# Two linear-attention and MLP layers on one core: the key chain regrouped, POOL's products held, norm turns moved into projections

## Chip, core and metric

The kernel runs on one core of a Trainium2 chip. The metric is the device time of one execution in microseconds (us); lower is better. Before the change the median of three executions is 2591.75 us (2591.71 to 2595.26).

Engines are called PE (TensorE, matmul; its weight loads are a row of their own, PEld), DVE (VectorE), ACT (ScalarE), POOL (GpSimd) and SP (SyncE, which issues the DMAs). PSUM holds matmul results, SBUF everything else. "L521" is line 521 of the kernel before; in the changed kernel the same statement stands 1 to 18 lines further down.

## Reference

The input x is 2048 x 576. Two layers with the same weights; 32 heads of width 18; the MLP is 4608 wide.

```python
def attention(x):                                  # x: [1, 2048, 576]
    q, k, v = heads(x @ wqkv)                      # each [1, 32, 2048, 18]
    pq, pk = q @ w_phi, k @ w_phi                  # per head, 18 x 18
    phi_q = concat([softmax(pq), softmax(-pq)])    # 36 features
    phi_k = concat([softmax(pk), softmax(-pk)])
    kv = phi_k^T v ; z = sum over rows of phi_k    # not causal: over all rows
    o = (phi_q kv) / (phi_q z + 1e-6)
    return merge(o) @ wo

def mlp(x):
    r = max(x @ w1 + b1, 0)
    return (r * r) @ w2 + b2

for _ in range(2):
    x = x + attention(layernorm(x))
    x = x + mlp(layernorm(x))
```

Since kv and z are sums over all rows, no query can be finished before the last key of its layer.

## The kernel before

**Arithmetic.** Every fp32 operand of a matmul is cut into a high and a low piece ("h" and "l": hi is the value cast, lo the rest), and a product is three matmuls: hi hi, hi lo, lo hi. The cuts are the small casts and subtractions on ACT, DVE and POOL throughout.

**Tiles.** The rows come in 4 blocks of 512 (TB), a block in 4 tiles of 128 rows; layer 0 has 16 key tiles K0 to K15. A projection of a tile is made in two halves of 288 columns (`half`).

**Order.** The program order on each engine is the order in which the code issues. Most stages fill a `Plan`: `plan.on(slot, depth, call)`; the slots are run in turn, and within a slot the calls of greater depth first. A slot is roughly one half projection of PE (14 matmuls). The barrier is written out by hand.

**Opening.** First `Fold` multiplies the feature weights w_phi into wqkv (`turn` = PE transposes L215 into "fp" and copies "ft", `times` = products "fo" L228, five chunks c), and `values` cuts the value weights of a chunk: hi on ACT (L254), lo on POOL (L255). Between these the first four row tiles get layer norm: `stats` (DVE bn_stats, then three small POOL operations L355, L356, L335 that make the scale and the shift), `scale` (ACT L344 and L345, which write the normed rows n_0n and n_0e) and `turn` (PE transposes L380 and L389, then cut into n_0h and n_0l by L381 and L382).

Then come the key tiles. For each T: two halves of k (PE, copied by ACT L445 into raw keys `ks`), `Keys.soften`, two halves of v, and `add`, the product kv += phi_k^T v (PE "kvp", L521), which needs the scaled exponentials of T. `soften` is five calls: peaks (DVE max and min, L457 and L458, and for T < 12 the second half of the difference on POOL, L471), difference (DVE L471), exponential (ACT L481), normalisers (DVE sum L484 and reciprocal L485), scale (DVE L494). Its table `at` gives slot and depth of each. The norm of the row tile four tiles ahead runs in the same slots, and in some of them `PrepareO` cuts the output weights ("or", "oh": ACT L296, DVE L297).

**Barrier** (`barrier`, once per layer). After the last key: the sums over heads are spread by matmuls (`key_totals`: "z", copied by ACT into zb) and kv is put into block form (`key_blocks`: transposes "kt", DVE products "ko", cut into kbh and kbl by `key_pieces`). Meanwhile PE projects queries of another block (`halves[1]` to `[7]`). The queries of four tiles Q0 to Q3 are then divided by their totals, two at a time, by `Weights`: `product` (E times zb, L594), `total` (sum, L599), `both` (L604 to L607, four small operations), `apply` (L494, scales E). The first pair is all on DVE, the second pair has its products on POOL. `heads` transposes the scaled queries (PE L630, "t0opt") and multiplies them by the key blocks (L651); `project` multiplies by wo (L674), and DVE adds to x (L677). Then the layer norm of the four tiles, whose transposed pieces (t0onh, t0onl in layer 0; t1onh, t1onl in layer 1) feed the MLP.

**MLP** (`g_mlp`, a generator; each `next(gen)` runs it up to its next `yield`). Feature block f of 128: `first` and `first2` bring weights (in the very first block of layer 0 raw, cut by ACT L765/L777 and POOL or DVE L766/L778), `hidden` is x @ w1 (L799), `square`, `second` (L817, L825). In the block behind a barrier ("apart") `hidden` is run on the first half of the rows (two tiles) before the other half is normed.

Of the kernel before, what the change touches and what calls it, by code (L numbers as in the profile page):

```python
# [7 lines left out]
F32 = mybir.dt.float32  # L8
# [5 lines left out]
P = 128  # L14
TB = 512
NT = TB // P
# [5 lines left out]
def layers_kernel(  # L22
# [78 lines left out]
    class Plan:  # L101
# [44 lines left out]
    nc.vector.tensor_copy(zero.rearrange("p (a b) -> p a b", a=2),  # L146
                          ident[0:1, P // 2 :].unsqueeze(1).to_broadcast([1, 2, P // 2]))
    zeros = zero[:, : 2 * DH].unsqueeze(1).to_broadcast([1, NS, 2 * DH])
    mhalf = cst.tile([P, 1], F32, name="mhalf")
    nc.vector.memset(mhalf, -0.5)  # L150
    b1t = cst.tile([P, NF], F32, name="b1t")
# [16 lines left out]
    class Fold:  # L168
# [81 lines left out]
        def values(self, c):  # L250
            for half in range(2):
                hi, lo = (piece[:, c] for piece in self.vpair[half])
                raw = self.vraws[c][:, half * HP : (half + 1) * HP]
                nc.scalar.activation(hi, raw, AF.Copy)  # L254
                nc.gpsimd.tensor_sub(lo, raw, hi.bitcast(F32))  # L255


# [290 lines left out]
    def key_blocks(layer):  # L548
        kv = sums[layer]["kv"]
        last, w = NG - 1, gw[-1]  # L550
        kbh = cst.tile([GW, 2, D], F32R, name=f"kbh{layer}", tag="kbh")
        kbl = cst.tile([GW, 2, D], F32R, name=f"kbl{layer}", tag="kbl")
        sums[layer]["kb"] = kbh, kbl
        own = sb.tile([P, KC * P], F32, tag="xn", name=f"kq{layer}")
        own = own[:, : 2 * w].rearrange("p (s q f) -> p s q f", s=2, q=NQ)
        nc.vector.tensor_mul(own, kv[:, :, HG].unsqueeze(2).to_broadcast([P, 2, NQ, DH]),
                             quarter.unsqueeze(1).unsqueeze(3).to_broadcast([P, 2, NQ, DH]))
        blocks, todo = own, []
        for s in range(2):
            pt = wtile(f"kt{layer}{s}")  # L560
            nc.tensor.transpose(pt[:GW, :P], kv[:, s, :HG].rearrange("p j f -> p (j f)"), ident)
            own = sb.tile([P, TB], F32, tag="hr", name=f"ko{layer}{s}", bufs=2)
            own = own[:GW, : NQ * GW].rearrange("p (q j d) -> p q j d", q=NQ, j=HG)
            src = pt[:GW, :P].rearrange("p (q d) -> p q d", q=NQ)[:, :, 1 : 1 + DH]
            nc.vector.tensor_mul(own, src.unsqueeze(2).to_broadcast([GW, NQ, HG, DH]),
                                 mask.unsqueeze(1).unsqueeze(3).to_broadcast([GW, NQ, HG, DH]))
            todo.append((own.rearrange("p q j d -> p (q j d)"), [k[:, s, : last * GW] for k in (kbh, kbl)]))
        pt = wtile(f"kt{layer}2")
        p3 = pt[:w, : 2 * w].rearrange("p (s n) -> p s n", s=2)
        for s in range(2):  # L570
            nc.tensor.matmul(p3[:, s], blocks[:, s].rearrange("p q f -> p (q f)"),
                             place.rearrange("p q d -> p (q d)"), start=True, stop=True)
        todo.append((p3, [k[:w, :, last * GW :] for k in (kbh, kbl)]))
        return todo

    def key_pieces(todo):
        for own, (hi, lo) in todo:
            nc.scalar.activation(hi, own, AF.Copy)
        for own, (hi, lo) in todo:
            nc.vector.tensor_sub(lo, own, hi.bitcast(F32))  # L580

# [165 lines left out]
    def g_mlp(layer, b, x, after, name, fresh, apart):  # L747
# [89 lines left out]
        if apart:  # L837
            for f in range(2):
                first(f, nc.gpsimd)
                first2(f, nc.gpsimd)  # L840
            yield
            for f in range(2):
                hidden(f, halves[0])
            yield
            for f in range(2):
                hidden(f, halves[1])
                square(f)
            yield
# [94 lines left out]
    class Keys:  # L943
# [41 lines left out]
        def add(self, T):  # L985
            kv_tile(self.layer, self.vts.pop(T), self.e.pop(T), f"{self.name}kv{T}")

        def soften(self, plan, T, raw, shared, at=((1, 1), (2, 2), (3, 3), (4, 4), (5, 5))):
            plan.on(raw + at[0][0], at[0][1], self.peaks, T, shared)
            for call, (k, depth) in zip((self.differences, self.exponential, self.normalisers, self.scale), at[1:]):  # L990
                plan.on(raw + k, depth, call, T)

    def barrier(layer, b, keys, queries, other, dst, out, gen):

        halves = [lambda t=t, h=h: other.half(t, h) for t in range(NT) for h in range(2)]
        keys()
        halves[1]()
        key_totals(layer)
        halves[2]()
        todo = key_blocks(layer)  # L1000
        weights = [Weights(layer, ([queries.e[t] for t in ts], queries.r[:, ts.start : ts.stop]),
                           f"{out.name}w{ts.start}") for ts in (range(0, 2), range(2, NT))]
        w = weights[0]
        w.product(0)
        w.total(0)
        halves[3]()
        w.product(1)
        key_pieces(todo)
        w.total(1)
        halves[4]()  # L1010
        w.both()
        halves[5]()
        w.apply(0)
        halves[6]()
        w.apply(1)
        halves[7]()
        out.ph = [queries.e[t] for t in range(NT)]
        for t in range(NT):
            out.load(t)
        w = weights[1]  # L1020
# [12 lines left out]
        next(gen)  # L1033
        w.total(0)
        w.total(1)
        out.project(0)
        w.both()
        w.apply(0)
        w.apply(1)
        out.project(1)  # L1040
        heads(1, 2)
        for t in range(2):
            norm.stats(t, out.x[t])
            norm.shift(t)
            norm.scale_by_act(t)
        for t in range(2, NT):
            out.project(t)
            norm.stats(t, out.x[t])
            norm.shift(t)
        spare["tags"] = [f"acc{i}" for i in range(NC)]  # L1050
        for t in range(2):
            norm.turn(t)
        norm.rest(0)
        for t in range(2, NT):
            norm.scale_by_act(t)
        next(gen)
        for t in range(2, NT):
            norm.turn(t)
        norm.rest(1)
        spare["tags"] = []  # L1060

# [7 lines left out]
    def opening():  # L1069
# [53 lines left out]
        for N in range(NT):  # L1123
            plan.on(3 * N + 1, 2, stats, N)
            plan.on(3 * N + 3, -1, scale, N)
            plan.on(3 * N + 4, -2, turn, N)
        for c, slot in enumerate((3, 5, 7, 9, 11)):
            plan.on(slot, -2, fold.values, c)
        first = NK - 2
# [215 lines left out]
```

## Time and profile before

| | us |
|---|---|
| median of 3 executions | 2591.75 |
| profiled execution | 2592.06 |
| its span, first to last instruction | 2590.1 |
| PE busy | 2529.3 |
| DVE busy | 1175.1 |
| ACT busy | 741.8 |
| POOL busy | 108.9 |

The mean granted clock of PE is 0.996 of full speed. Layer 0's opening fold fills about the first 30 us, the key tiles the stretch from 30 to 215, its barrier 213 to 271; layer 1's barrier is at about 1490 to 1550. The rest is MLP and the attention of other blocks woven into it, where PE is busy nearly throughout.

In a list of waits a row reads: engine, its waiting instruction's output and line, "<-" the engine, output and line that came last, then us in total, times, longest. In a timeline a row is start, duration, engine, line, operation, out<-in with shapes; in brackets the idle time of that engine just before, and what ended it.

### The profile page before, as it was taken

The numbers are of one execution on the slowest core, as the hardware profiler recorded it, in microseconds if no ns is written. First come the engines' busy times: TensorE is split into PE (matmuls) and PEld (weight loads), VectorE is DVE, ScalarE is ACT, GpSimd is POOL, SyncE is SP. The second block draws the span as 40 slices with busy tenths as digits, with TensorE's granted clock in tenths as the row PEclk, the third lists the DMA queues.
The fourth block names the chain that finished last, engine by engine and source line by source line (L and its number), as shares of the span: only waits on it lengthen the run. The fifth ranks groups of instructions, "written<-read, shape, count | busy, mean of one in ns | idle before, by whom it ended". The sixth has DMA issues, their size and how long they took to land.

```text
span 2590.1 us, 37314 instructions
## 1 busy us (share of the span) xinstructions
PE 2529.3 (98%) x15300; PEld 2222.6 (86%) x15300; DVE 1175.1 (45%) x1985; ACT 741.8 (29%) x1278; POOL 108.9 (4%) x261
## 2 busy tenths in 40 slices
PE   8888999999999999999999989999999999999999
PEld 8888788888888888888888978888888888888887
DVE  5678775444543445434312676332263326332112
ACT  5433443422221222312222332212222222222221
POOL 3211000000000000000000010000000000000000
PEclk9999999999999999999999999999999999999999
DMA  9404586886656766565566217556654674556655
GB/s 316 155 20 142 188 278 222 276 306 230 199 199 209 240 239 200 165 224 186 184 196 210 100 51 231 162 180 223 226 164 145 193 267 153 164 175 227 197 194 172
DMA packets 161143, 505.47 MB, mean 195 GB/s; under 512 B 21334, under 2 KB 49526, under 8 KB 160974
## 3 DMA queue, kind: packets, MB, share of 16 engines
q1 hardware_dynamic: 160974, 503.10, 58.4%
q8 instruction: 121, 1.98, 0.3%
q14 instruction: 48, 0.39, 0.0%
HBM read 418.39 MB, written 84.64 MB: 194 GB/s over the span
## 4 chain that ended last, share of the span: by engine, by line
PE 85%; DVE 6%; ACT 2%; DMA 2%; issue 1%; POOL 1%; SPq 0%; DVEq 0%; ACTq 0%
PE m_1ph L799 9%; PE m_0ph L799 9%; PE m_2ph L799 9%; PE m_3ph L799 7%; PE m_1acc L825 7%; PE m_0acc L825 7%; PE m_2acc L825 7%; PE m_3acc L825 6%; PE m_1acc L817 2%; PE m_0acc L817 2%; PE m_2acc L817 2%; PE m_3acc L817 2%; DMA m_3rr<-in_B_w 2%; PE a_2po L674 1%; PE a_0po L674 1%
## 5 line engine op out<-in xcount | busy, mean ns | idle before, releaser
L799 PE MATMUL m_0ph<-a_0nh,m_0h 128*128 128x512 f32 x720 | 226.2, 396 | 0.0
L799 PE MATMUL m_2ph<-a_2nh,m_2h 128*128 128x512 f32 x720 | 225.5, 395 | 0.3 <-DMA m_2h<-dw 0.3
L825 PE MATMUL m_3acc<-m_3s,m_3hb 128*128 128x448 f32 x864 | 189.6, 367 | 0.4 <-DVE m_3hb L809 0.4
L825 PE MATMUL m_1acc<-m_1s,m_1hb 128*128 128x448 f32 x864 | 189.5, 367 | 0.4 <-PE m_1ph L799 0.4
L825 PE MATMUL m_0acc<-m_0s,m_0hb 128*128 128x448 f32 x864 | 189.9, 368 | 0.0
L825 PE MATMUL m_2acc<-m_2s,m_2hb 128*128 128x448 f32 x864 | 189.6, 367 | 0.0
L825 PEld LDWEIGHTS m_1acc<-m_1s,m_1hb 128*128 128x128 f32 x864 | 161.6, 188 | 18.3 <-PE m_1ph L799 0.5
L825 PEld LDWEIGHTS m_3acc<-m_3s,m_3hb 128*128 128x128 f32 x864 | 161.3, 188 | 17.8 <-PE m_3ph L799 0.6
L825 PEld LDWEIGHTS m_2acc<-m_2s,m_2hb 128*128 128x128 f32 x864 | 160.6, 188 | 16.0
L809 DVE CAST m_2hb<-m_2hr 128x512 fp32r<-128x512 f32 x72 | 30.8, 427 | 315.9 <-ACT m_2hr L806 315.5
L825 PEld LDWEIGHTS m_0acc<-m_0s,m_0hb 128*128 128x128 f32 x864 | 160.3, 188 | 15.5
L799 PEld LDWEIGHTS m_2ph<-a_2nh,m_2h 128*128 128x128 f32 x720 | 135.3, 188 | 31.1 <-issue 0.7
L799 PEld LDWEIGHTS m_0ph<-a_0nh,m_0h 128*128 128x128 f32 x720 | 135.3, 188 | 29.9
L809 DVE CAST m_1hb<-m_1hr 128x512 fp32r<-128x512 f32 x72 | 30.7, 427 | 270.1 <-ACT m_1hr L806 270.1
L805 ACT ACTIVATE m_2hr<-m_2ph,b1t 128x512 f32<-128x512 f32 x72 | 49.6, 689 | 351.9 <-PE m_2ph L799 351.9
L809 DVE CAST m_0hb<-m_0hr 128x512 fp32r<-128x512 f32 x72 | 30.8, 427 | 260.8 <-ACT m_0hr L806 260.4
L805 ACT ACTIVATE m_0hr<-m_0ph,b1t 128x512 f32<-128x512 f32 x72 | 49.6, 689 | 333.4 <-PE m_0ph L799 333.4
L805 ACT ACTIVATE m_1hr<-m_1ph,b1t 128x512 f32<-128x512 f32 x72 | 49.6, 689 | 324.2 <-PE m_1ph L799 324.2
L799 PE MATMUL m_3ph<-t0onh,m_3h 128*128 128x512 f32 (+1 forms) x380 | 116.3, 390 | 6.7 <-ACT m_3hr L805 3.9
L799 PE MATMUL m_1ph<-t1onh,m_1h 128*128 128x512 f32 (+1 forms) x380 | 114.2, 384 | 1.0 <-ACT t1onh L381 1.0
L799 PE MATMUL m_3ph<-a_3nh,m_3h 128*128 128x512 f32 x360 | 113.1, 396 | 0.0
L799 PE MATMUL m_0ph<-a_0nl,m_0h 128*128 128x512 f32 x288 | 113.0, 392 | 0.0
(1930 smaller groups left out, 5506.9 us busy)
## 6 DMA issues: line engine op xcount, KB each, us to landing
m_2h<-dw SPq DMA_DIRECT2D x72, 640.0 KB
m_0h<-dw SPq DMA_DIRECT2D x72, 640.0 KB
m_1h<-dw SPq DMA_DIRECT2D x72, 640.0 KB
m_2s<-dw SPq DMA_DIRECT2D x72, 576.0 KB
m_0s<-dw SPq DMA_DIRECT2D x72, 576.0 KB
m_1s<-dw SPq DMA_DIRECT2D x72, 576.0 KB
dw<-m_3h SPq DMA_DIRECT2D x36, 640.0 KB
m_3h<-dw SPq DMA_DIRECT2D x36, 640.0 KB
```

Of the source, the lines that this page charges most:

```text
L674: nc.tensor.matmul(pt[:, :HP], a, m[:w, g], start=(g == 0 and k == 0), stop=(g == NG - 1 and k == 2))
L799: nc.tensor.matmul(ph[:, cols], a, m, start=(k == 0), stop=(k == 3 * KC + 1))
L805: nc.scalar.activation(hr, ph, AF.Relu, bias=b1t[:, f : f + 1])
L809: nc.vector.tensor_copy(hh, hr)
L817: nc.tensor.matmul(acc[KC], a, m, start=(f == 0 and k == 0), stop=(f == NF - 1 and k == 2))
L825: nc.tensor.matmul(acc[t][:, :R], a[:, rows], m, start=(f == 0 and k == 0), stop=(f == NF - 1 and k == 2))
```

## The change

1. `Keys.soften` has another table: the difference directly behind the peaks in the same slot, and the exponential, normalisers and scale ahead of the other work of their slots, the scale one slot earlier. `between` (layer 1) uses the same table.
2. In the opening fold `values` casts hi on POOL too (before: ACT), and each norm turn comes one slot later.
3. In the barrier `key_blocks` is issued before `key_totals`, apart from its last part (`own_blocks`), which follows them; `key_pieces` is split: `key_highs` (ACT) after the first total, `key_lows` (DVE, kbl) between the two `apply` calls. `apply(0)` is issued before `halves[5]`.
4. `hold(e)` copies one column of e to a tile `gate` on POOL. Since e is written by `apply`, POOL's later instructions start only after that `apply`. It stands before the second pair's products and before the first MLP step, and that step (`next(gen)`) moves from before `total(0)` of the second pair to after its `apply(1)`.
5. At the barrier's end, turn(0) and turn(1) of the norm stand between the two halves of `project(3)`, turn(2) between the two `hidden` calls of the MLP's first half of rows, turn(3) after them.

```diff
+    gate = cst.tile([P, 1], F32, name="gate")
...
-                nc.scalar.activation(hi, raw, AF.Copy)
+                nc.gpsimd.tensor_copy(hi, raw)
                 nc.gpsimd.tensor_sub(lo, raw, hi.bitcast(F32))
...
         blocks, todo = own, []
+
+        def own_blocks():
...
+            todo.append((p3, [k[:w, :, last * GW :] for k in (kbh, kbl)]))
+            return todo
+
         for s in range(2):
             pt = wtile(f"kt{layer}{s}")
...
-        return todo
-
-    def key_pieces(todo):
+        return own_blocks
+
+    def key_highs(todo):
         for own, (hi, lo) in todo:
             nc.scalar.activation(hi, own, AF.Copy)
+
+    def key_lows(todo):
         for own, (hi, lo) in todo:
             nc.vector.tensor_sub(lo, own, hi.bitcast(F32))
...
             for f in range(2):
                 hidden(f, halves[0])
-            yield
+                yield
...
-        def soften(self, plan, T, raw, shared, at=((1, 1), (2, 2), (3, 3), (4, 4), (5, 5))):
+        def soften(self, plan, T, raw, shared, at=((1, 2), (1, 1.5), (2, 3), (3, 4), (4, 5))):
...
+    def hold(e):
+        nc.gpsimd.tensor_copy(gate, e[:, 0, 0:1])
...
         halves[1]()
+        own_blocks = key_blocks(layer)
         key_totals(layer)
+        todo = own_blocks()
         halves[2]()
-        todo = key_blocks(layer)
...
         w.product(0)
         w.total(0)
+        key_highs(todo)
         halves[3]()
         w.product(1)
-        key_pieces(todo)
         w.total(1)
         halves[4]()
         w.both()
+        w.apply(0)
         halves[5]()
-        w.apply(0)
+        key_lows(todo)
+        w.apply(1)
         halves[6]()
-        w.apply(1)
         halves[7]()
...
+        hold(queries.e[1])
         w = weights[1]
         w.product(0, nc.gpsimd)
         w.product(1, nc.gpsimd, True)
...
         norm = Norm(dst, f"{out.name}n")
-        next(gen)
         w.total(0)
         w.total(1)
         out.project(0)
         w.both()
         w.apply(0)
         w.apply(1)
+        hold(queries.e[3])
+        next(gen)
         out.project(1)
         heads(1, 2)
...
-        for t in range(2, NT):
-            out.project(t)
-            norm.stats(t, out.x[t])
-            norm.shift(t)
+        out.project(2)
+        norm.stats(2, out.x[2])
+        norm.shift(2)
         spare["tags"] = [f"acc{i}" for i in range(NC)]
+        out.project(3, (0,))
         for t in range(2):
             norm.turn(t)
+        out.project(3, (1,))
         norm.rest(0)
-        for t in range(2, NT):
-            norm.scale_by_act(t)
+        norm.scale_by_act(2)
+        norm.stats(3, out.x[3])
+        norm.shift(3)
+        norm.scale_by_act(3)
         next(gen)
-        for t in range(2, NT):
-            norm.turn(t)
+        norm.turn(2)
+        next(gen)
+        norm.turn(3)
         norm.rest(1)
...
-            plan.on(3 * N + 4, -2, turn, N)
+            plan.on(3 * N + 5, -2, turn, N)
```

What this makes of the order on DVE around key tile K4 (s0K4m holds its peaks, s0K4e the differences and exponentials, n_1 and n_2 are the norms of row blocks 1 and 2), before:

```order
L457 TENSOR_REDUCE s0K4m<-s0ks_1170 128x32
L458 TENSOR_REDUCE s0K4m<-s0ks_1170 128x32
L382 TENSOR_TENSOR n_1l<-n_1p_1237,n_1h 128x4x128
L391 TENSOR_TENSOR n_1h<-n_1p_1244,n_1h 64x256
L353 BN_STATS n_2s_1253<-x_8_995 128x6 x2
L354 BN_AGGR n_2m_1254<-n_2s_1253 128x2
L471 TENSOR_TENSOR s0K4e<-s0ks_1170,s0K4m 128x576
L297 TENSOR_TENSOR or_928<-or_928,oh_1206 72x288
L484 TENSOR_REDUCE s0K4r<-s0K4e 128x64
L485 RECIPROCAL s0K4r<-s0K4r 128x64
L494 TENSOR_TENSOR s0K4e<-s0K4e,s0K4r 128x1152
```

and now:

```order
L458 TENSOR_REDUCE s0K4m<-s0ks_1174 128x32
L459 TENSOR_REDUCE s0K4m<-s0ks_1174 128x32
L472 TENSOR_TENSOR s0K4e<-s0ks_1174,s0K4m 128x576
L383 TENSOR_TENSOR n_1l<-n_1p_1239,n_1h 128x4x128
L392 TENSOR_TENSOR n_1h<-n_1p_1246,n_1h 64x256
L354 BN_STATS n_2s_1256<-x_8_997 128x6 x2
L355 BN_AGGR n_2m_1257<-n_2s_1256 128x2
L298 TENSOR_TENSOR or_930<-or_930,oh_1208 72x288
L485 TENSOR_REDUCE s0K4r<-s0K4e 128x64
L486 RECIPROCAL s0K4r<-s0K4r 128x64
L495 TENSOR_TENSOR s0K4e<-s0K4e,s0K4r 128x1152
```

The difference of K4 stands directly behind its peaks, ahead of the norm's n_1l and statistics n_2s; the tail of "or" stands ahead of the sum in both.

DVE in barrier 0, from the key blocks to the scaling of Q1, before:

```order
L565 TENSOR_TENSOR ko_3003<-kt_3001,mask 126x504
L565 TENSOR_TENSOR ko_3007<-kt_3005,mask 126x504
L594 TENSOR_TENSOR t0ow0m_3012<-t0q3Q0e,zb_2961 128x1152
L599 TENSOR_REDUCE t0ow0u<-t0ow0m_3012 128x64
L594 TENSOR_TENSOR t0ow0m_3032<-t0q3Q1e,zb_2961 128x1152
L580 TENSOR_TENSOR kbl_2998<-ko_3003,kbh_2997 126x504
L580 TENSOR_TENSOR kbl_2998<-ko_3007,kbh_2997 126x504
L580 TENSOR_TENSOR kbl_2998<-kt_3009,kbh_2997 72x2x72
L599 TENSOR_REDUCE t0ow0u<-t0ow0m_3032 128x64
L604 TENSOR_TENSOR t0ow0u<-t0ow0u,t0q3r 128x128
L605 SCALAR_TENSOR_TENSOR t0ow0u<-t0ow0u 128x2x32
L606 RECIPROCAL t0ow0u<-t0ow0u 128x2x32
```

and now:

```order
L601 TENSOR_TENSOR t0ow0m_3013<-t0q3Q0e,zb_2974 128x1152
L606 TENSOR_REDUCE t0ow0u<-t0ow0m_3013 128x64
L601 TENSOR_TENSOR t0ow0m_3036<-t0q3Q1e,zb_2974 128x1152
L606 TENSOR_REDUCE t0ow0u<-t0ow0m_3036 128x64
L611 TENSOR_TENSOR t0ow0u<-t0ow0u,t0q3r 128x128
L612 SCALAR_TENSOR_TENSOR t0ow0u<-t0ow0u 128x2x32
L613 RECIPROCAL t0ow0u<-t0ow0u 128x2x32
L614 TENSOR_TENSOR t0q3r<-t0q3r,t0ow0u 128x128
L495 TENSOR_TENSOR t0q3Q0e<-t0q3Q0e,t0q3r 128x1152
L587 TENSOR_TENSOR kbl_2963<-ko_2968,kbh_2962 126x504
L587 TENSOR_TENSOR kbl_2963<-ko_2972,kbh_2962 126x504
L587 TENSOR_TENSOR kbl_2963<-kt_2993,kbh_2962 72x2x72
```

The three subtractions into kbl left the place between the products of Q0 and Q1 and their sums; they stand behind the scaling of Q0.

POOL in barrier 0, from the products of the second pair to the cuts of the MLP's first weights (m_3h, m_3s), before:

```order
L594 TENSOR_TENSOR t0ow2m_3121<-t0q3Q2e,zb_2961 128x1152
L594 TENSOR_TENSOR t0ow2m1e<-t0q3Q3e,zb_2961 128x1152
L766 TENSOR_TENSOR m_3h_0_3233<-m_3rr_3234,m_3h_0_3233 128x640
L778 TENSOR_TENSOR m_3s_0_3242<-m_3rr_3234,m_3s_0_3242 128x576
L766 TENSOR_TENSOR m_3h_1_3246<-m_3rr_3247,m_3h_1_3246 128x640
L778 TENSOR_TENSOR m_3s_1_3255<-m_3rr_3247,m_3s_1_3255 128x576
```

and now:

```order
L1001 COPY gate<-t0q3Q1e 128x1
L601 TENSOR_TENSOR t0ow2m_3123<-t0q3Q2e,zb_2974 128x1152
L601 TENSOR_TENSOR t0ow2m1e<-t0q3Q3e,zb_2974 128x1152
L1001 COPY gate<-t0q3Q3e 128x1
L773 TENSOR_TENSOR m_3h_0_3279<-m_3rr_3280,m_3h_0_3279 128x640
L785 TENSOR_TENSOR m_3s_0_3288<-m_3rr_3280,m_3s_0_3288 128x576
L773 TENSOR_TENSOR m_3h_1_3292<-m_3rr_3293,m_3h_1_3292 128x640
L785 TENSOR_TENSOR m_3s_1_3301<-m_3rr_3293,m_3s_1_3301 128x576
```

Two one-column copies into the gate are added: the first reads Q1's scaled exponentials ahead of the products, the second Q3's ahead of the cuts.

More of the change, by code (lines that the diff above doesn't have):

```diff
@@ L558, in key_blocks @@
         blocks, todo = own, []
+        def own_blocks():
+            pt = wtile(f"kt{layer}2")
+            p3 = pt[:w, : 2 * w].rearrange("p (s n) -> p s n", s=2)
+            for s in range(2):
+                nc.tensor.matmul(p3[:, s], blocks[:, s].rearrange("p q f -> p (q f)"),
+                                 place.rearrange("p q d -> p (q d)"), start=True, stop=True)
+            todo.append((p3, [k[:w, :, last * GW :] for k in (kbh, kbl)]))
+            return todo
         for s in range(2):
@@ L567, in key_blocks @@
             todo.append((own.rearrange("p q j d -> p (q j d)"), [k[:, s, : last * GW] for k in (kbh, kbl)]))
[L568 to L573, printed above, removed]
-        return todo
-    def key_pieces(todo):
+        return own_blocks
+    def key_highs(todo):
         for own, (hi, lo) in todo:
             nc.scalar.activation(hi, own, AF.Copy)
+    def key_lows(todo):
         for own, (hi, lo) in todo:
```

## Prediction

> **What bounds the kernel now.** I read the page first: busy shares, then the chain that ended last.
>
> ```profile
> PE 2529.3 (98%) x15300; PEld 2222.6 (86%) x15300; DVE 1175.1 (45%) x1985; ACT 741.8 (29%) x1278; POOL 108.9 (4%) x261
> ...
> PE 85%; DVE 6%; ACT 2%; DMA 2%; issue 1%; POOL 1%; SPq 0%; DVEq 0%; ACTq 0%
> ```
>
> TensorE (PE) works 2529.3 us of a span of 2590.1, so only 60.8 us of idle PE, and what a low clock costs it, can be had; VectorE (DVE) is next in the chain. Nothing here shortens PE's own work, so the forecast is a list of PE's idle places that the change touches. The table of windows finds them (span, then busy time and count of PE, PE's loads, DVE, ACT, POOL, then granted clock, DMA share, GB/s):
>
> ```profile
> core 0: us, PE busy (x) PEld busy (x) DVE busy (x) ACT busy (x) POOL busy (x), PEclk, DMA share, GB/s
> 0.00:30.00 30.00, 22.39 (x161) 19.49 (x162) 17.68 (x49) 19.56 (x51) 13.56 (x35) 1.00 0.91 263
> 60.00:90.00 30.00, 25.61 (x367) 24.82 (x367) 20.26 (x32) 11.61 (x23) 8.25 (x18) 1.00 0.54 180
> 90.00:180.00 90.00, 75.87 (x1081) 73.63 (x1080) 64.50 (x93) 36.16 (x74) 19.57 (x48) 0.98 0.25 81
> 220.00:230.00 10.00, 8.04 (x61) 7.80 (x60) 9.79 (x11) 3.25 (x8) 3.45 (x2) 1.00 0.29 92
> 230.00:240.00 10.00, 5.79 (x30) 5.34 (x31) 7.45 (x10) 3.07 (x9) 1.80 (x1) 0.66 0.55 182
> 240.00:260.00 20.00, 17.35 (x131) 15.85 (x129) 18.05 (x34) 9.49 (x25) 5.95 (x4) 1.00 0.55 188
> 1500.00:1520.00 20.00, 13.84 (x93) 12.78 (x92) 16.89 (x25) 6.27 (x17) 5.25 (x2) 0.83 0.34 125
> ```
>
> Idle PE is 7.61 us in 0-30 (opening fold), 4.39 + 14.13 = 18.52 us in 60-180 (the sixteen key tiles of layer 0), 1.96 + 4.21 + 2.65 in 220-260 (barrier 0) and 6.16 in 1500-1520 (barrier 1). In 230-240 the clock was 0.66, in 1500-1520 it was 0.83. These places hold 39 of the 60.8 us.
>
> **Key chain.** PE's waits in 60-180, the first and the last of 12 rows, longest first:
>
> ```profile
> PE kvp L521 <- DVE s0K3e L494: 2.3, 1, 2.3
> ...
> PE kvp L521 <- DVE s0K1e L494: 0.2, 1, 0.2
> ```
>
> All twelve are at the key product L521, eleven of them for DVE's scaling of the exponentials (K1 to K12 but for one, which names an ACT copy); their sum is the 18.52 of the windows. DVE over one key tile, K3:
>
> ```profile
> 71.57 0.74 DVE L457 TENSOR_REDUCE s0K3m<-s0ks 128x32 f32<-128x576 f32 x1
> ...
> 74.46 0.70 DVE L471 TENSOR_TENSOR s0K3e<-s0ks,s0K3m 128x576 f32<-128x576 f32 x1
> 78.61 1.35 DVE L484 TENSOR_REDUCE s0K3r<-s0K3e 128x64 f32<-128x1152 f32 x1 [3.44 <-ACT s0K3e L481]
> ...
> 81.68 1.35 DVE L494 TENSOR_TENSOR s0K3e<-s0K3e,s0K3r 128x1152 f32<-128x1152 f32 x1
> ```
>
> From the peaks to the end of the scaling (81.68 + 1.35) is 11.4 us, of which DVE idles 3.44 waiting for ACT's exponential. ACT and POOL show why:
>
> ```profile
> 76.31 0.82 ACT L344 ACTIVATE n_1n<-x,n_1b,n_1d 128x512 f32<-128x512 f32 x1 [5.96 <-POOL n_1b L335]
> ...
> 77.36 1.15 ACT L481 ACTIVATE s0K3e<-s0K3e 128x1152 f32<-128x1152 f32 x1
> ```
>
> ```profile
> 73.11 1.17 POOL L471 TENSOR_TENSOR s0K3e<-s0K3m,s0ks 128x576 f32<-128x576 f32 x1 [7.13 <-issue]
> ```
>
> The exponential stands behind the norm's n_1n, which waits 5.96 us for POOL's statistics; those need DVE's statistics, which stand ahead of DVE's own difference (74.46), though POOL's half of it began at 73.11. After the change the difference follows the peaks directly and the exponential precedes n_n. From 71.57: to the start of POOL's half at 73.11 1.54 (two peaks and a hand-over), both differences side by side until POOL's ends, 1.17, hand-over 0.1, exponential 1.15, hand-over 0.1, then the totals, reciprocal and scaling, 78.61 to 83.03 less about 1.2 for L297, which now stands behind, 3.2: about 7.3 us. DVE's other work of the cycle, n_l and the statistics (between the peaks and 74.46, 1.5), now fills part of its wait. With a long L297 in a tile DVE needs up to 8.5. PE needs 11.4 minus its wait of 2.3, about 9.1 us per tile. DVE is then shorter than PE in every tile, and the waits end: its lag does not build up, because each tile leaves 0.6 to 1.8 us over. What is late next is the norm: n_1n now waits for the exponential as well. The statistics come 0.6 us later behind the difference, and n_1n starts some 0.6 to 1.5 us later against the peaks; but the peaks start at least the 2.3 of L521's wait earlier against PE, since the raw keys no longer wait for DVE to finish the tile before. So the transposes stay covered; uncovered, 1 us late each would cost 12. I take 18.0 of the 18.52 (bounds 9, the first rival's, and 18.6), leaving part of the wait that an ACT copy owns.
>
> One page speaks against this. The Trainium skill, "SBUF — State Buffer", section "Who interferes with whom", says that a VectorE instruction with two SBUF inputs and a GpSimd instruction that reads SBUF exclude each other for the whole instruction. The differences of DVE and POOL, now adjacent, are such a pair. By it POOL's half would start some 0.4 us later, or DVE's 1.2 later, and the sum would lose nothing or about 3 us (the first rival).
>
> **Barriers.** PE waits in 220-260, then in 1500-1540:
>
> ```profile
> PE t0opt L630 <- DVE t0q3Q0e L494: 5.4, 1, 5.4
> PE t0opt L630 <- DVE t0q3Q2e L494: 1.6, 1, 1.6
> PE t0opt L630 <- DVE t0q3Q3e L494: 0.9, 1, 0.9
> PE t0opt L630 <- DVE t0q3Q1e L494: 0.7, 1, 0.7
> ```
>
> ```profile
> PE t1opt L630 <- DVE t1qQ0e L494: 5.4, 1, 5.4
> PE t1opt L630 <- DVE t1qQ1e L494: 0.7, 1, 0.7
> ```
>
> They are the transposes L630 that wait for the scaled queries. DVE ahead of that (first half of the weights in barrier 0), POOL beside it, and the same L605 in barrier 1's second half, where POOL was idle:
>
> ```profile
> 218.42 1.27 DVE L565 TENSOR_TENSOR ko<-kt,mask 126x504 f32<-126x504 f32 x2 [3.46 <-PE kt L561]
> ...
> 223.65 1.27 DVE L580 TENSOR_TENSOR kbl<-ko,kbh 126x504 fp32r<-126x504 f32 x2
> ...
> 226.76 2.55 DVE L605 SCALAR_TENSOR_TENSOR t0ow0u<-t0ow0u 128x64 f32<-128x64 f32 x1
> ...
> 229.93 2.01 DVE L607 TENSOR_TENSOR t0q3r<-t0q3r,t0ow0u 128x128 f32<-128x128 f32 x1
> 231.98 1.36 DVE L494 TENSOR_TENSOR t0q3Q0e<-t0q3Q0e,t0q3r 128x1152 f32<-128x1152 f32 x1
> ...
> 248.74 1.34 DVE L605 SCALAR_TENSOR_TENSOR t0ow2u<-t0ow2u 128x64 f32<-128x64 f32 x1
> ```
>
> ```profile
> 226.55 2.68 POOL L594 TENSOR_TENSOR t0ow2m<-t0q3Q2e,zb 128x1152 f32<-128x1152 f32 x1 [56.56 <-DVE t0ow0u L599]
> ```
>
> ```profile
> 1521.17 0.23 DVE L605 SCALAR_TENSOR_TENSOR t1ow2u<-t1ow2u 128x64 f32<-128x64 f32 x1
> ```
>
> L605 takes 2.55 with POOL's product running and 0.23 without; L607, twice its elements, takes 2.01, against an unstalled 0.3 by estimate. So the stall is 2.32 + 1.7 = 4.0 us, and `hold` removes it: POOL starts only after the second `apply`. kbl (1.27 for two of its three pieces, 1.4 in all by estimate) leaves the way to Q0e. The key blocks ahead of the totals close the 3.46 us of waiting at 218.42 partly: the blocks are cut while PE forms the totals, and the first product then waits for zb instead; I take 2.3 (bounds 1.0 and 3.46). Q0e was ready at 231.98 + 1.36 = 233.3; 4.0 + 1.4 + 2.3 = 7.7 gives 225.6, and Q1e, behind kbl, 1.3 + 1.4 later, 228.4. PE ran out at 228.04 (busy 8.04 in 220-230). So Q0e costs nothing and Q1e about 0.3: of 5.4 + 0.7 go 5.8. Without that gap the clock should stay full: (1 - 0.66) x 5.79 = 2.0 us in 230-240; I take 1.8. In barrier 1 it is the same gap and the same lock, (1 - 0.83) x 13.84 = 2.3, again 1.8 taken.
>
> The second weights of barrier 0 wait 1.6 + 0.9: there POOL's cuts of the MLP's first weights stood beside L604 and L605; the row at 248.74 took 1.34 instead of 0.23, and L604 ahead of it by estimate as much longer: 2.2 us. The second `hold` moves those cuts behind the last `apply`. I take 2.0 (bounds 0 and 2.5). In barrier 1 the second half had no such stall and gains 0.
>
> What is queued behind the holds: POOL's two products (2.68 each) begin at about 228.6 and end near 234. DVE's totals of them stand behind the first heads' work, which PE runs without the gap from 228 for about 8 us (5.79 in 230-240, at the low clock, and what spills over): 2 us over. The cuts take 5.95 us of POOL (its row of 240-260) and now start after the second scaling; the second heads and half of the projections, by estimate 15 us of PE, stand between that and their use. The SP loads of the next weights wait for those cuts and shift with them.
>
> **Norm rows.** The last norm tiles of each block are turned between projections or half-blocks of the MLP instead of together. Waits of barrier 0:
>
> ```profile
> PE m_3ph L799 <- DVE t0onl L382: 1.2, 2, 0.7
> PE m_3ph L799 <- ACT t0onh L381: 1.0, 2, 0.5
> ```
>
> 2.2 us, twice (barrier 1 has the same two rows). A transpose with a whole piece of PE work behind it hides its copy and its subtraction; the last one, turn(3) and the rest, stays exposed. I take 1.0 per barrier (bounds 0 and 2.2).
>
> **Opening fold.** PE waits in 0-30, the ACT copy that moves, and POOL's row of the same shape:
>
> ```profile
> PE n_0p L380 <- ACT n_0n L344: 3.8, 4, 1.3
> PE fo L228 <- ACT ft L220: 1.6, 4, 0.5
> ```
>
> ```profile
> 11.27 0.43 ACT L254 ACTIVATE w0v0h<-fv 128x288 fp32r<-128x288 f32 x1
> ```
>
> ```profile
> 11.78 0.79 POOL L255 TENSOR_TENSOR w0v0l<-fv,w0v0h 128x288 fp32r<-128x288 f32 x1 [2.78 <-ACT w0v0h L254]
> ```
>
> Both waits are for ACT. Ten copies of 0.43 leave it, some 0.33 each where they follow one another, 0.66 per chunk, so 2.6 over the four chunks that have such waits; the norm turn one slot later fills part of the 3.8. I take 2.5 of 5.4 (bounds 0 and 5.4). The copy on POOL has no row: its nearest is the two-input subtraction of the same shape, 0.79, the upper end, and a quarter of it, 0.2, the lower; I take 0.6. POOL's 13.56 us of the first 30 become 19.6; it holds. The Trainium skill, "GPSIMD Engine Reference", section "4.1 Engine selection", calls one-input work there roughly line-rate and two-input work about twice VectorE's time; by that, an estimate of 0.4, the sum would be the same.
>
> **The sum.** -18.0 (keys) - 2.5 (fold) - 5.8 - 1.8 - 2.0 - 1.0 (barrier 0: first gap, clock, second half, norm) - 5.8 - 1.8 - 1.0 (barrier 1) = -39.7. From the profiled execution's own 2592.06, 0.3 above the median of 2591.75: 2552.4. I say 2553. With every upper bound (18.6, 5.4, and 2.0, 2.5, 2.2 and 2.3, 2.2 with gaps of 6.1) it is 47.4 off, 2545 at the least.
>
> **The rivals.** The lock moves into the keys: DVE's difference waits out POOL's each time. For it: L605's 2.55, and that both now start within 0.2 us of each other. Against: the one that starts first is DVE's, and there is slack. Tiles with a long L297 (8.5 + 1.2 = 9.7 against 9.1) would lose 0.6 each, four of them 2.4 us, and a late POOL delays n_n and the transposes in all twelve; with half of the key gain lost, 9 us, 2561.
>
> The barriers give only half: the totals' zb, not the stall, may end last, and a shorter gap may still drop the clock. Half of 7.6 in each is 7.6: 2560.
>
> The fold is bound by POOL: a copy of 1.6, twice the subtraction, makes 13.56 + 16 = 29.6 of the first 30 us; its last chunk ends some 4 us late and the values' first product waits: 2556 to 2557.
>
> The fresh MLP is bound by DMA, which is nearly full there:
>
> ```profile
> 300.00:340.00 40.00, 38.86 (x176) 32.43 (x175) 33.90 (x52) 18.67 (x27) 0.00 (x0) 1.00 0.90 305
> ```
>
> PE idles only 1.14 in it, and loads are released by work that moves along with PE; against it stands that the loads before 260 do not come earlier. It would swallow at most barrier 0's 10.6: 2563.
>
> Slower: the norm's transposes in the keys. If n_n came later than the slot of its transpose in all twelve tiles, PE would wait there instead of at L521. It ends above 2592.1 from 39.7 / 12 = 3.3 us of net wait each, that is, n_n some 5 us later than I work out; at 4 us each, 2600. POOL's chain (n_n's releaser) would have to double for it; POOL is busy 19.57 of 90 us.
>
> The change doing nothing: only if PE's order shifted the waits to the next instruction, for which no row speaks.
>
> **How the numbers follow.** My case 0.62 (2546 to 2558), lock in the keys 0.12, half barriers 0.10, fold on POOL 0.05, DMA 0.06, slower 0.03, nothing 0.02. 2545 to 2568 leaves out the last two and the far parts of the others, about 0.15. A difference of 0.2% (5 us) is what a measurement of this kernel can tell from none: faster 0.95, same 0.02, slower 0.03.
>
> **What the profile after would show.** L521 without waits for DVE in 60-180, PE over 29 of 30 us there; L605 and L607 at 0.2 to 0.3 in both barriers, POOL's products after the second scaling; granted clock 1.0 at the first heads; t0onh and t0onl with half their waits; fold windows with PE at 25 of 30. I am wrong if L380 in the keys waits for n_n, if DVE's difference takes 1.9 there, if POOL's copies take over 1.5, or if PE idles over 3 us in the fresh MLP.

## The result

| | before, us | after, us |
|---|---|---|
| median (lowest to highest) of 4 executions | 2591.73 (2591.1 to 2595.26) | 2547.67 (2543.99 to 2548.95) |
| profiled execution | 2592.06 | 2546.92 |
| its span | 2590.1 | 2544.8 |

The ratio after/before is 0.9825 (95% interval 0.9808 to 0.9842): faster by 44 us, 5 more than forecast, inside the range. One execution further down, of the run with the old norm order, took 3074.73 us at a granted clock of 0.754 and is left out of that run's median. The page of after, busy shares and chain:

```profile
PE 2518.6 (99%) x15300; PEld 2215.2 (87%) x15300; DVE 1166.4 (46%) x1985; ACT 741.9 (29%) x1268; POOL 112.9 (4%) x275
...
PE 94%; DVE 2%; DMA 2%; ACT 1%; issue 1%; SPq 0%; POOL 0%; DVEq 0%; ACTq 0%; POOLq 0%
```

PE's idle time fell from 60.8 to 26.2 us (2544.8 less 2518.6), and PE's busy time itself from 2529.3 to 2518.6 with the same 15300 matmuls. Of the 45.3 us of span, 34.6 are idle time and 10.7 are busy time. Of the 10.7, stretches at half clock explain 7.7: before, PE worked 15.4 us in such stretches, and after, none (mean granted clock 0.996 and 1.000). The other 3.0 I have not placed. Windows of after (columns as before: the second figure is PE's busy time, the third from the end the clock):

```profile
0.00:30.00 30.00, 23.11 (x177) 20.97 (x178) 18.00 (x50) 17.30 (x43) 17.45 (x45) 1.00 0.93 258
60.00:90.00 30.00, 30.00 (x403) 29.38 (x402) 24.34 (x36) 16.02 (x31) 8.96 (x20) 1.00 0.66 210
90.00:180.00 90.00, 90.00 (x1203) 88.12 (x1202) 79.15 (x110) 42.49 (x79) 16.65 (x42) 1.00 0.22 70
200.00:210.00 10.00, 9.89 (x76) 8.91 (x75) 8.40 (x19) 5.46 (x17) 5.43 (x3) 1.00 0.80 258
210.00:230.00 20.00, 18.88 (x142) 17.56 (x140) 16.64 (x37) 9.03 (x22) 8.12 (x11) 1.00 0.43 154
300.00:340.00 40.00, 37.40 (x172) 30.88 (x170) 30.30 (x47) 17.10 (x26) 0.00 (x0) 1.00 0.84 283
```

PE no longer idles at all from 30 to 200, and the clock is full throughout. One key tile of after: DVE, ACT and POOL around K4 (lines are 1 higher than before).

```profile
74.92 0.75 DVE L458 TENSOR_REDUCE s0K4m<-s0ks 128x32 f32<-128x576 f32 x1
...
76.24 0.75 DVE L472 TENSOR_TENSOR s0K4e<-s0ks,s0K4m 128x576 f32<-128x576 f32 x1
...
82.21 1.36 DVE L495 TENSOR_TENSOR s0K4e<-s0K4e,s0K4r 128x1152 f32<-128x1152 f32 x1
83.48 0.75 DVE L458 TENSOR_REDUCE s0K5m<-s0ks 128x32 f32<-128x576 f32 x1
```

```profile
78.05 1.17 ACT L482 ACTIVATE s0K4e<-s0K4e 128x1152 f32<-128x1152 f32 x1 [2.74 <-DVE n_1h L392]
...
80.50 0.82 ACT L345 ACTIVATE n_2n<-x,n_2b,n_2d 128x512 f32<-128x512 f32 x1 [0.66 <-POOL n_2b L336]
```

```profile
76.47 1.54 POOL L472 TENSOR_TENSOR s0K4e<-s0K4m,s0ks 128x576 f32<-128x576 f32 x1 [7.15 <-DVE s0K4m L459]
...
79.22 0.22 POOL L356 TENSOR_SCALAR n_2d<-n_2m 128x1 f32<-128x1 f32 x1 [1.10 <-DVE n_2m L355]
```

The difference (76.24) follows the peaks, the exponential (78.05) starts when POOL's half is done and 2.45 us ahead of n_2n (80.50), and DVE hardly waits for it. From the peaks (74.92) to the end of the scaling is 8.7 us, with the small piece of "or" inside; before it was 11.0 in this tile. In K3, the tile of the prediction, it is 7.7 (forecast 7.3) where it was 11.4. The next peaks start at 83.48, right behind the scaling, and PE has no idle time here.

Barrier 0 of after on DVE and POOL, then all of PE's listed waits in 180 to 260 but one of 0.4 in the MLP:

```profile
192.12 1.36 DVE L601 TENSOR_TENSOR t0ow0m<-t0q3Q0e,zb 128x1152 f32<-128x1152 f32 x1 [0.74 <-ACT zb L547]
...
198.00 0.22 DVE L612 SCALAR_TENSOR_TENSOR t0ow0u<-t0ow0u 128x64 f32<-128x64 f32 x1
...
198.85 0.29 DVE L614 TENSOR_TENSOR t0q3r<-t0q3r,t0ow0u 128x128 f32<-128x128 f32 x1
199.18 1.36 DVE L495 TENSOR_TENSOR t0q3Q0e<-t0q3Q0e,t0q3r 128x1152 f32<-128x1152 f32 x1
...
201.86 1.35 DVE L495 TENSOR_TENSOR t0q3Q1e<-t0q3Q1e,t0q3r 128x1152 f32<-128x1152 f32 x1
```

```profile
203.35 0.19 POOL L1001 COPY gate<-t0q3Q1e 128x1 f32<-128x1 f32 x1 [55.05 <-DVE t0q3Q1e L495]
203.49 2.65 POOL L601 TENSOR_TENSOR t0ow2m<-t0q3Q2e,zb 128x1152 f32<-128x1152 f32 x1
```

```profile
PE t0onp L381 <- ACT t0onn L345: 0.6, 1, 0.6
PE t0opo L681 <- DVE t0ox L684: 0.6, 1, 0.6
PE t0opt L637 <- DVE t0q3Q3e L495: 0.5, 1, 0.5
PE m_3ph L806 <- ACT t0onh L382: 0.5, 1, 0.5
PE m_3ph L806 <- DVE t0onl L383: 0.4, 1, 0.4
```

L612 and L614 (L605 and L607 before) take 0.22 and 0.29; POOL's gate copy and products start behind the scaling of Q1. The transposes t0opt wait for Q0e and Q1e no more. In the fold PE's waits are of another kind, and the cast on POOL has its row now:

```profile
PE fo L229 <- DVE ft L219: 4.7, 4, 1.8
```

```profile
9.78 0.43 POOL L255 CAST w0v0h<-fv 128x288 fp32r<-128x288 f32 x1
```

Stage by stage, from starts of the same instructions in the two traces (us). The key blocks' two transposes, 0.2 us, now stand ahead of "z" and count in the key stage:

| from, to | before | after | gained | forecast |
|---|---|---|---|---|
| first fold product, first key matmul | 29.23 | 27.25 | 2.0 | 2.5 |
| first key matmul, first "z" of barrier 0 | 177.50 | 155.03 | 22.5 | 18.0 |
| that "z", first L825 of the MLP | 67.43 | 56.65 | 10.8 | 10.6 |
| from there to the gap of barrier 1 | 1221.04 | 1219.80 | 1.2 | 0 |
| barrier 1, gap included, to the MLP's first L825 | 50.36 | 41.74 | 8.6 | 8.6 |

### The profile page after: what moved, and what is told of

It reads as the page before. It is cut to its first block, busy times and chain, and to the rows that moved or that the text cites. A ratio compares the mean times of both kernels' runs of the same rounds, so it can differ in the third digit from the quotient of the medians.

```text
span 2544.8 us, 37319 instructions
## 1 busy us (share of the span) xinstructions
PE 2518.6 (99%) x15300; PEld 2215.2 (87%) x15300; DVE 1166.4 (46%) x1985; ACT 741.9 (29%) x1268; POOL 112.9 (4%) x275
## 4 chain that ended last, share of the span: by engine, by line
PE 94%; DVE 2%; DMA 2%; ACT 1%; issue 1%; SPq 0%; POOL 0%; DVEq 0%; ACTq 0%; POOLq 0%
PE m_0ph L806 9%; PE m_2ph L806 9%; PE m_1ph L806 9%; PE m_3ph L806 7%; PE m_0acc L832 7%; PE m_1acc L832 7%; PE m_2acc L832 7%; PE m_3acc L832 6%; PE m_1acc L824 2%; PE m_0acc L824 2%; PE m_2acc L824 2%; PE m_3acc L824 2%; DMA m_3rr<-in_B_w 1%; PE a_2po L681 1%; PE a_0po L681 1%
```

## The experiments

Each run is the changed kernel with one part undone or altered. Times are medians of four executions, lowest and highest in brackets. Where parts of one stage are compared, the length of that stage in the trace decides, since totals of one kernel spread over 1 to 6 us.

**Keys: the whole table back.** `at=((1, 1), (2, 2), (3, 3), (4, 4), (5, 5))`.

> The changed kernel with the old table of Keys.soften. If the table alone frees the keys, the waits at the key product come back whole: 18.5 us of idle PE, the 1.3 us of low clock at 90-100 us and 1.5 at K13 to K15, so 2547.7 + 21 to 22.3 = 2569 to 2570. If the later norm turn of the opening or POOL's relief did part of it, the loss is under 15 us, 2562 or less.

2570.71 us (2567.46 to 2573.81), 23.0 above the changed kernel. The key stage is 177.7 us, as before the change (177.5). The table is the whole gain of that stage.

**Keys: only the difference early.**

```diff
-at=((1, 2), (1, 1.5), (2, 3), (3, 4), (4, 5))
+at=((1, 2), (1, 1.5), (3, 3), (4, 4), (5, 5))
```

> The changed kernel with half of the new table: the difference directly behind the peaks, but exponential, normalisers and scale in their old slots, so the exponential stands behind n_n again. Theory A, the exponential's place behind n_n is the whole cost: from the peaks 1.3 + 0.7 + 0.6 + 1.0 on DVE, 1.2 on POOL, 1.1 of n_n, then the exponential 1.1, sum at +7.1 us, where it was at +7.0 before; no gain from the difference, 2567 to 2570. Theory B, the difference standing behind the statistics was half of it: about 2558.

2570.80 us (2570.58 to 2573.07). DVE and ACT around K3 in this run:

```profile
71.52 0.75 DVE L458 TENSOR_REDUCE s0K3m<-s0ks 128x32 f32<-128x576 f32 x1
...
72.85 0.75 DVE L472 TENSOR_TENSOR s0K3e<-s0ks,s0K3m 128x576 f32<-128x576 f32 x1
```

```profile
76.53 0.81 ACT L345 ACTIVATE n_1n<-x,n_1b,n_1d 128x512 f32<-128x512 f32 x1 [6.56 <-POOL n_1b L336]
...
77.59 1.15 ACT L482 ACTIVATE s0K3e<-s0K3e 128x1152 f32<-128x1152 f32 x1
```

Theory A. DVE's half of the difference is done 1.5 us earlier after the peaks than before (2.1 instead of 3.6), POOL's half at 3.1, and the exponential starts 6.1 us after the peaks all the same (before: 5.8), behind n_1n and its 6.56 us of waiting for POOL. The key stage is 179.6 us, 1.9 longer than with the whole old table; PE idles about as much in both (19.0 and 18.6), and this run has three stretches at half clock there, the other two. So the early difference by itself gives nothing. The rest of the table (exponential, sums and scaling ahead of other work) gives the gain. By the traces of K3 that is mainly the exponential, 3.1 us after the peaks in the changed kernel instead of 6.1, and then "or", 1.2 us, which no longer stands between sums and scaling. These places were not run one by one, and no run has them without the early difference.

**Keys: no POOL beside DVE.** `ks.soften(plan, T, raw, False)`: both differences on DVE.

> The changed kernel with both halves of the keys' differences on DVE, so that no POOL work stands beside DVE's. In the changed kernel POOL's half takes 1.55 us where it took 1.17. If that lock costs nothing (PE sets the pace with 1 to 2 us to spare per tile): waits at the key product stay 0, 2547 to 2549. If it is what is left over in the keys, nothing can be seen there, since PE idles 0.0 in 60-180; so a gain is excluded, and a loss of 0.5 us in tiles with a long L298 (DVE 0.7 more per tile) is the other outcome: up to 2 us.

2547.98 us (2546.55 to 2550.0), the key stage 155.2 against 155.0, no waits:

```profile
60.00:180.00 120.00, 120.00 (x1660) 117.27 (x1660) 108.18 (x155) 58.30 (x111) 12.05 (x54) 1.00 0.32 106
```

The lock of the first rival is there: POOL's half took 1.17 and takes 1.55 beside DVE's. It costs nothing, and taking it away gains nothing, since PE has no idle time left.

**Barriers: no holds.** Both `hold` calls left out.

> The changed kernel without the two gate copies on POOL; all else stays. Theory A, the stall of DVE beside POOL's products is worth its 4.0 us in each barrier and 2.0 more in barrier 0's second half: the small operations L612 and L614 at 2.5 and 2.0 us again, PE waits about 4 us, in two pieces under 3 us each, the clock stays at 1.0: 2547.7 + 10 = 2557 to 2558. Theory B, the gap also drops the clock: 2 to 3 us more, 2560 to 2561. Theory C, the key blocks' earlier place has already taken the gap and the holds give nothing: 2548 to 2550.

2560.53 us (2558.56 to 2564.02), 12.9 above. DVE's two operations, PE's waits and two stretches at half clock in barrier 0 (profiled execution: 2564.02):

```profile
199.28 2.59 DVE L612 SCALAR_TENSOR_TENSOR t0ow0u<-t0ow0u 128x64 f32<-128x64 f32 x1
...
202.49 2.08 DVE L614 TENSOR_TENSOR t0q3r<-t0q3r,t0ow0u 128x128 f32<-128x128 f32 x1
```

```profile
PE t0opt L637 <- DVE kbl L587: 2.9, 1, 2.9
PE t0opt L637 <- DVE t0q3Q2e L495: 1.6, 1, 1.6
PE t0opt L637 <- DVE t0q3Q3e L495: 0.9, 1, 0.9
PE t0opt L637 <- DVE t0q3Q1e L495: 0.8, 1, 0.8
```

```profile
207.33:214.16 6.83, 5.96 (x27) 5.49 (x27) 4.11 (x9) 2.73 (x8) 0.00 (x0) 0.50 0.68 224
227.81:234.64 6.83, 6.37 (x29) 6.19 (x30) 4.62 (x12) 3.45 (x9) 0.00 (x0) 0.50 0.58 177
```

The stall is as forecast: 2.59 + 2.08 instead of 0.22 + 0.29. The first row of the waits names kbl: these transposes started at 207.42, although Q0e was ready at 205.96. They write the PSUM tile that held "kt": the kernel takes seven such tiles in turn here, and six half projections lie between. So they wait for the last reader of kt, the third piece of kbl, which ended at 207.36.

Theory B, and stronger than it said. Barrier 0 is 10.7 us longer than after. The waits shown are 5.7 more (2.9 + 0.8 + 1.6 + 0.9, less the 0.5 that the changed kernel has), and waits of 1.5 at the norm rows are gone. The clock costs 6.2: half of the 5.96 and 6.37 us that PE worked in the two stretches. Together that is 10.4. Barrier 1 is 5.0 longer.

**Barriers: the old place of the key blocks.** Holds kept; `key_blocks`, `key_highs`, `key_lows` and both `apply` where they stood.

> The changed kernel with the holds kept, but key blocks, their pieces and the applies in the old order. By the durations of the trace the first product starts 2.8 us later and kbl stands 1.5 us ahead of the first scaling: Q0e 4.3 and Q1e 2.9 us later, PE waits about 1.8 + 0.9 in each barrier, clock 1.0: 2547.7 + 5.5 = 2553. If the holds alone had removed the gap: 2548 to 2549.

2557.25 us (2557.15 to 2557.93), 9.6 above, more than the 5.5 expected.

```profile
PE t0opt L637 <- DVE t0q3Q0e L495: 1.3, 1, 1.3
PE t0opt L637 <- DVE t0q3Q1e L495: 0.9, 1, 0.9
```

```profile
210.00:220.00 10.00, 10.00 (x75) 9.62 (x74) 8.20 (x17) 6.30 (x15) 2.58 (x1) 0.93 0.18 72
1470.00:1480.00 10.00, 7.74 (x50) 7.16 (x50) 7.73 (x16) 4.09 (x12) 5.26 (x3) 0.83 0.68 249
```

The waits are 1.3 + 0.9, nearly as worked out (1.8 + 0.9); the stages are 4.3 and 3.3 longer. The rest is the clock, which the expectation had full: one stretch of 3.41 us at half clock in each barrier, from 208.01 and from 1474.35, behind two gaps of 1.3 to 1.4 and 0.9 us. They show as 0.93 and 0.83 in the rows and cost 1.7 and 1.6 us.

**Barriers: both undone.**

> The changed kernel without the gate copies and with the key blocks, their pieces and the applies in the old order. If the two parts add up with the clock: 6.0 us of PE wait and 1.2 to 1.8 of clock in each barrier, 1.8 in barrier 0's second half, 2547.7 + 16 to 17.5 = 2564 to 2565; granted clock about 0.83 in the 20 us around each gap. If the clock loss has another cause: 2561 and clock 1.0.

2567.91 us (2567.53 to 2568.95), 20.2 above. The old gap is back whole:

```profile
PE t0opt L637 <- DVE t0q3Q0e L495: 5.4, 1, 5.4
...
PE t0opt L637 <- DVE t0q3Q1e L495: 0.7, 1, 0.7
```

Barrier 0 is 11.7 us longer than after, barrier 1 8.4; the change gained 10.8 and 8.6 there. The two parts don't add up: alone they cost 15.7 (no holds) and 7.5 (old place) of barrier time, together 20.1. With either part alone undone smaller gaps remain, and much of the clock's cost with them: counted as half of PE's work in the stretches at half clock, 7.8 us over both barriers without holds and 3.3 with the old place, against 6.7 with both undone.

**Norm turns in the old order.**

> The changed kernel with the norm's turns at the end of each barrier in the old order. My sum had 1.0 us for each barrier; the two traces' first matmuls suggest 0.5 to 0.7. So 2549 to 2550, waits for t0onh and t0onl at 2.2 us together again instead of 0.9, and the waits of 0.6 for n_n and 0.6 for the adds to x gone.

Median 2549.3 us (2547.51 to 2551.09); against 2547.67 no measurable difference. By the trace barrier 0 is 0.3 longer and barrier 1 1.0; other executions of the same barriers at full clock agree to about 0.1. Turning early takes 1.3 of the 2.2 us of waits for t0onh and t0onl. In barrier 0 nearly all of that goes back as the waits of 0.6 for n_n and 0.6 for the sum into x, in barrier 1 only the first 0.6.

**Fold: the casts back on ACT.**

> The changed kernel with the value weights' high casts back on ACT; the norm turn of the opening stays one slot later. Counted from the first product of the fold to the first key matmul, the changed kernel took 27.25 us, the kernel before 29.23. If the casts carried the gain, this is 28.9 to 29.3; if the later turn did, 27.3 to 27.6; half each, about 28.2. The total moves by no more than 2 us (and 1.2 for the clock's dip that this stage has in some executions): 2547 to 2551.

2547.20 us (2545.8 to 2547.36): not to be told apart in the total. The fold is 29.58 us, but in this execution the clock was 0.83 in 20 to 30. In five executions of the changed fold that dip cost 1.2 to 1.3; without it this run has about 28.3, by estimate, against 27.25 and 29.23. So about half of the fold's gain is the casts'. The other half falls to the later turn, which was not run alone.

**Fold: transposes first in their slots.** `plan.on(k, 2, fold.turn, k)`.

> The changed kernel with the opening fold's transposes (and their copies ft) ahead of the products of the same slot instead of behind. PE now waits 4.7 us for DVE's ft in the fold; if only ft's place in DVE's order makes it late, it is ready 1 to 1.5 us earlier per chunk, and 2 to 4.5 us go: the keys' first matmul at 30 to 32 us instead of 34.0, 2544 to 2546. If ACT's and DVE's turn-taking on the pieces sets the pace, nothing changes: 34.0 and 2548.

2546.49 us (2545.19 to 2547.66); the fold takes 27.83 and not 27.25. But PE ran at half clock in this execution until about 11 us: the first eight products of the fold took 1.91 us here and 1.16 in the changed kernel.

```profile
7.08 1.91 PE L229 MATMUL fo<-phi,ft 126*128 126x126 f32 x8
```

```profile
6.71 1.16 PE L229 MATMUL fo<-phi,ft 126*128 126x126 f32 x8 [0.68 <-DVE ft L219]
```

The run with the old norm order has the changed kernel's fold with the same slow start (2.08 for eight products): its fold takes 29.17. Against that this run is 1.3 shorter, or 0.9 by the first key matmul (34.91 against 35.79), and PE's listed waits for ft are 2.4 instead of 4.2. So ft's place in DVE's order is part of the wait, about 1 us of it, where 2 to 4.5 were expected.

**Fold: ft on ACT.** The DVE copy of `turn` goes to ACT.

> The changed kernel with all ft copies on ACT, none on DVE. ft would start behind the last hi piece at once, some 0.3 us earlier per chunk, but n_n behind it 0.5 us later: 1 to 1.5 us gained in the fold (keys' first matmul at 32.5 to 33) if DVE's ft is the pace, 0 to 2 lost if ACT is.

2544.86 us (2543.61 to 2547.18), the fold 26.83: 0.4 better, less than expected. The first key matmul stands at 33.05 instead of 33.96, since the first product, too, starts 0.5 earlier (6.22).

**Fold: high pieces first.**

```diff
             for hi, lo, at in parts:
                 m = hi.shape[-1]
                 nc.scalar.activation(hi, po[:, at : at + m], AF.Copy)
+            for hi, lo, at in parts:
+                m = hi.shape[-1]
                 nc.vector.tensor_sub(lo, po[:, at : at + m], hi.bitcast(F32))
```

> The changed kernel with the fold's pieces cut in another order: both high pieces of a product on ACT first, then both low pieces on DVE, instead of high, low, high, low. Theory: ACT and DVE wait for each other at the second piece (ACT 0.53 to 1.14 us for w0k0l, DVE 0.42 for w0k1h, once per chunk, and again for the 72-wide pieces), and ft stands behind that. About 0.6 to 0.9 us less per chunk: from the first product to the first key matmul 23.5 to 25 instead of 27.25, 2543 to 2545. If PE's own work or the loads bound the fold, 27.2 and 2548.

2545.28 us (2544.3 to 2546.12), the fold 25.32: 1.9 better, just beyond the slow end of the expectation (25). PE waits less for ft, and now for loads:

```profile
PE fp L216 <- DMA fr<-in_A_wqkv: 2.4, 3, 1.0
PE fo L229 <- DVE ft L219: 1.5, 2, 0.8
```

**Fold: high pieces first and ft on ACT.**

> As the run before it, with the ft copies all on ACT as well. If ACT then is the pace (its busy time of about 17.3 us in the first 30 grows by 3), no better than the run before: 24 to 26 us for the fold; if ft behind DVE's pieces still was the pace, 23 to 24 and 2542 to 2544.

2542.40 us (2541.12 to 2544.44), the fold 24.84:

```profile
PE fp L216 <- DMA fr<-in_A_wqkv: 2.5, 3, 1.8
PE fo L227 <- ACT ft L219: 0.3, 1, 0.3
```

Of PE's listed waits, what is left is the loads. Ratio to the kernel before: 0.9802 (0.9787 to 0.9817), against 0.9825 (0.9808 to 0.9842) for the change; by the trace of the fold it is 2.4 us better than the changed kernel, by the first key matmul 3.0 (30.93 against 33.96), and by medians 5.

## Why the prediction was right, and where its sizes were off

- **Keys** (18.0 forecast, 22.5 measured): the two table runs show that the table is the gain, and that the difference alone is not; the exponential's place behind n_n is the larger part by the traces. The term was mis-sized because I counted idle PE in 60 to 180 only (18.5). The waits of K14, K15 and the first "z" (1.3 together) went too, and a stretch of 3.41 us at half clock, all of it work (1.7); 1.0 more I can't place.
- **The lock as rival**: it happened (1.55 for 1.17) and was hidden, as the slack per tile said; the run without POOL shows it. The slack was larger than my 0.6 to 1.8: from the end of the scaling to its product L522 it is 1.6 to 5.0 us in K1 to K11. The Trainium skill, "SBUF — State Buffer", section "Who interferes with whom", has the rule right: L612 beside POOL's products took 2.59, alone 0.22; and the sum over the last axis, which it says never contends, took 1.34 beside POOL's cuts of weights in barrier 0 before the change and 1.34 alone after it.
- **Barriers** (10.6 and 8.6 forecast, 10.8 and 8.6 measured): right in sum, and partly by luck, since in barrier 0 the sizes offset each other. There the waits at the transposes gave 8.1 (7.8 forecast), the clock 2.3 (1.8), and the norm 0.3 (1.0). The parts are not separable as I listed them. I charged the clock 1.8 per barrier as a companion of the one gap of 5.4; the runs show it behind shorter gaps too, so that the holds alone would have left half of the clock's cost, and the new place alone all of it. I also took kbl off the way to Q0e; the run without holds shows that the first transposes still wait for kbl's last piece, through the PSUM tile. In the changed kernel that piece ends at 201.94, and PE arrives at 203.10, so it costs nothing.
- **Holds**: nobody waits behind them. POOL's products (203.5 to 208.8) are done before DVE's sums of them at 210.9, 2.1 us over, as forecast.
- **Norm turns** (1.0 per barrier): 0.3 and 1.0 by the trace; not visible in the total. I left out the new waits for n_n and for the sum into x.
- **Fold** (2.5): 2.0 in the profiled execution. The casts took 0.43, I had taken 0.6; the estimate of 0.4 from the Trainium skill's "GPSIMD Engine Reference", section "4.1 Engine selection", was the better one. What sets the pace next I had not worked out. It is not POOL but ft, which PE waits 4.7 us for: cutting both high pieces first takes 1.9 us off, and ft's place in DVE's order about 1. PE reached 23.1 of 30 us, not 25.
- **DMA in the fresh MLP**: the part of the MLP that ran in 300 to 340 before, where PE idled 1.14, runs in 264.75 to 304.75 now, and PE idles 1.15 there. (In 300 to 340 of after, a later part, it is 2.6.) In the 100 us behind the MLP's first L825 it idles 4.6, where before it was 3.9, so the rival took 0.7 at most of the 10.6 that it could have swallowed. The stretch from there to barrier 1 is 1.2 shorter all the same; a stretch at half clock at 508.5 us is in the trace before only.

## What to carry to other kernels

Where an engine idles for another's result, ask what stands ahead of that result in the other engine's program: here one exponential behind a norm step that waited for a third engine was the larger part of a wait of 1.2 to 2.3 us of PE in each of nine tiles (K2 to K4 and K6 to K11), and the step had slack. Hold a helper engine's large operation until the small ones on the critical path are through, if the two exclude each other. And count a PE gap by more than its length: closing only part of it may leave the clock's share of the loss standing.

## What I had not expected of the hardware

The clock falls behind gaps that are short, and what counts is how a gap falls into windows of time. Between the start and the end of these runs every stretch at half clock is 3.41 us long, or twice that, and the starts of such stretches in one trace lie whole multiples of 3.41 us apart (84.58, 118.71 and 139.19 in the run with only the difference early: 10 and 6 windows). So the trace can be cut into windows of 3.41 us. Two waits of the kernel before, at K3 (2.33 us, ending at 83.17) and at K4 (2.11 us, ending at 94.09), the columns as before (the second figure is PE's busy time, the third from the end the clock):

```profile
78.43:81.84 3.41, 2.41 (x20) 2.17 (x17) 3.20 (x4) 3.39 (x9) 0.00 (x0) 1.00 0.55 164
81.84:85.25 3.41, 2.08 (x74) 2.07 (x75) 3.38 (x5) 0.00 (x0) 0.76 (x1) 1.00 0.94 343
92.08:95.49 3.41, 1.40 (x69) 1.39 (x70) 3.38 (x5) 0.34 (x1) 0.07 (x1) 1.00 0.49 124
95.49:98.90 3.41, 3.41 (x16) 3.41 (x15) 1.93 (x5) 0.30 (x1) 2.66 (x6) 0.50 0.49 192
```

The longer wait is split by the border of two windows (1.0 and 1.3 us idle), and the clock stays full. The shorter one lies in one window (2.0 us idle), and the next window runs at half clock. Over the fourteen traces, without their first microseconds and their end, 15 windows at full clock had 2.0 us or more of idle PE, and half clock followed all 15. Of 6974 with less than 1.3 us it followed none; of the 41 between, 15. What decides between 1.3 and 2.0 us stays open. The changed barriers lie there, too: in three executions of the later runs their three small waits, 1.5 us together in one window, were followed by half clock, and the barrier took 1.0 to 1.3 us longer.

This accounts for the fold. Eight of these runs have the same fold, with PE waits of up to 1.85 us. In five of the profiled executions the clock was about 0.83 in 20 to 30, and the fold took 28.5 us. In three it was 1.00, and the fold took 27.2 in two of them and 29.2 in the third, which ran at half clock until about 10.7 us. The Trainium skill, "TensorE: Matmul & The Clock Gate", section "What's actually happening", puts the fall behind at least one idle window of about 3.4 us. The length of the window agrees with the 3.41 here, but a window need not be idle throughout: 2.0 us of idle time in it was enough.

POOL's small statistics operation took 0.61 us before and 0.22 after in the keys, since DVE's difference no longer runs beside it: the lock did not vanish, it moved from the statistics to POOL's half of the difference.
